# Keys, queries and tokens turned by DMAs instead of TensorE, with the transfers placed around them

## Chip, cores, metric

One core of one Trainium2 chip. The metric is the device time of one execution in microseconds; each figure is a median of several runs, and runs are compared in the fast state only. The "span" of a profile runs from its first instruction to its last and is 1.5 to 2 us shorter than the time. The engines are TensorE (PE; its weight loads PEld), VectorE (DVE), ScalarE (ACT), GpSimd (POOL) and SyncE (SP), which here only issues DMAs.

## The reference, cut

```python
# q, k, v: (4 batches, 8 heads, 768, 64); mem_k, mem_v: (4, 8, 8, 64)
for c in range(24):                              # chunks of 32 queries
    k_ctx = k[:, :, max(0, 32*c - 16) : min(768, 32*c + 40)]   # 16 left, 8 right; v_ctx alike
    scores = q_c @ concat(mem_k, k_ctx).T / 8
    out[c] = softmax(scores) @ concat(mem_v, v_ctx)
x = out as (4, 768, 512)
y = x + relu(((x - mean) / sqrt(var + 1e-6) * g_ln) @ w_ch1) @ w_ch2      # 512 -> 2048 -> 512
```

## The kernel before

The 3072 tokens are worked on as 24 tiles of 128, three tiles to a **unit**; batch b is units 2b and 2b + 1. A unit is 28 steps: 16 up steps (`up`, four matmuls of `w_ch1`, then a ReLU that DVE and ACT take in turn) and 12 down steps (`down`, four matmuls of `w_ch2`). Between them stands the attention of the next unit. A table says behind which step each piece is issued; every engine is given its instructions in this order. An instruction that waits holds up those behind it: in the changed kernel (below) DVE stood 6.6 us before one copy, and the ReLU behind that copy, for which TensorE waited 4.5 us, ran only after it.

The matmuls of this program read three things turned from rows to columns: keys and queries of each batch, and the normalised tokens of each tile. The kernel before does all of it on TensorE, through PSUM, with a copy by DVE or ACT behind each turn:

```python
def turn_kq(pv, src, j, n):              # keys or queries: two heads of a batch
    for r in range(8):
        for par in range(2):
            nc.tensor.matmul(out=pv[64*par : 64*par+64, n*r : n*r+n], lhsT=src[0:n, 2*j+par, r, :],
                             rhs=identity[0:n, 0:n], is_transpose=True, ...)

def turn_x(u, i, t, kind="att"):         # one tile of normalised tokens
    pv = ...                             # PSUM
    for dt in range(4):
        nc.tensor.matmul(out=pv[:, 128*dt : 128*dt+128], lhsT=xn[t % 3][:, 128*dt : 128*dt+128],
                         rhs=identity, is_transpose=True, ...)
    nc.scalar.copy(out=xT[u % 2][:, :, 128*i : 128*i+128], in_=...)
```

Its plan for the units that matter (cut):

```python
elif u in (2, 4):
    attend(((1, 8, 8, 12), (4, 8, 10, 14), (11, 17, 17, 21)))   # scores, values, norm, token turn
    b = u // 2 + 1
    for j, step in ((0, 17), (2, 23)):
        at(step, kq_block, b, j, 0, NG, "mm")                   # keys and queries of batch b
        ...
    for h in range(H):
        at(2 + 2 * h, load_v_head, b, h)                        # values of batch b
    at(21, mem_cols, b); at(21, v_mem, b); at(22, v_around, b)
elif following:
    attend(((12, 17, 17, 21), (14, 17, 17, 22), (18, 23, 23, 26)))
    if u == 3: ...                                              # loads of keys and queries, batch 3
```

`v_around` copies, in SBUF, the rows that neighbouring groups share; it needs all eight value loads.

The softmax here doesn't subtract the row's maximum and nothing guards it: scores larger than these inputs give would overflow.

## Time and profile before

| | before |
|---|---|
| time | 231.92 us (231.57 to 233.25, 3 runs) |
| TensorE busy | 222.8 of 230.2 us |
| units 2 to 6 | 27.1, 24.1, 27.1, 24.1, 24.1 us, TensorE idle 0.0 in each |
| granted clock | 1.0 throughout |

A unit's length is taken from its first up matmul to that of the next. With TensorE idle 0.0 us in units 2 to 6, the account below takes what was removed from it at its length there and each new wait at its own.

### The profile page before, as it was taken

To read this page: it belongs to the slowest core of one execution; us is meant where nothing else is said; L and a number is where in the kernel's file an instruction comes from. 1 tells how busy PE (TensorE), PEld (TensorE's weight loads), DVE (VectorE), ACT (ScalarE), POOL (GpSimd) and SP (SyncE) were. 2 spreads that over 40 slices of the span, in tenths; PEclk is the share of its full clock that TensorE was granted. 3 is DMA by queue.
4 is the path that set the end of the run, shared out by engine and by line. 5 is a ranking of instruction groups with operands and counts; after the bars stand their busy time and mean duration, and the time that the engine had idled before them with its cause. 6 is when DMAs were issued, how large, how long until landed. Compare 5 with 4: busy or idle time off the path is not lost.

```text
span 230.2 us, 5499 instructions
## 1 busy us (share of the span) xinstructions
PE 222.8 (97%) x2289; PEld 138.2 (60%) x2289; DVE 125.4 (54%) x290; ACT 119.0 (52%) x228; POOL 68.6 (30%) x125
## 2 busy tenths in 40 slices
PE   7989999899999999999999999999999999999993
PEld 2455776447765577555765577556765566557553
DVE  5746881475747639575336648674436542663222
ACT  3565648253894576655355367654356335534200
POOL 6973343877360380530001370410001200030000
PEclk9999999999999999999999999999999999999999
DMA  5999999999999999548921199543001200111012
GB/s 80 169 90 203 201 211 150 125 200 226 121 69 126 226 145 36 37 77 119 236 48 48 48 127 23 37 99 106 0 3 46 90 4 0 47 48 46 0 48 93
DMA packets 50307, 21.91 MB, mean 95 GB/s; under 512 B 37817, under 2 KB 46777, under 8 KB 50234
## 3 DMA queue, kind: packets, MB, share of 16 engines
q0 software_dynamic: 45680, 14.23, 90.1%
q1 hardware_dynamic: 4602, 7.33, 10.5%
q8 instruction: 18, 0.29, 0.6%
q14 instruction: 7, 0.06, 0.1%
HBM read 28.48 MB, written 6.29 MB: 151 GB/s over the span
## 4 chain that ended last, share of the span: by engine, by line
PE 77%; DMA 16%; POOL 2%; DVE 2%; issue 1%; POOLq 0%
PE mm L319 32%; PE mm L336 32%; DMA w2c<-in_moe_w_ch_dram 13%; PE att L238 4%; DMA V<-in_v_dram 3%; PE att L258 3%; PE att L176 3%; PE att L296 2%; POOL V L114 2%; PE mm L354 2%; PE mm L176 1%; DVE QZ L374 1%; DVE V L379 0%; DVE V L378 0%; DVE osb L359 0%
## 5 line engine op out<-in xcount | busy, mean ns | idle before, releaser
L319 PE MATMUL mm<-xT,w1c 128*128 128x384 f16 x512 | 88.3, 326 | 0.0
L336 PE MATMUL mm<-w2c,rT 128*128 128x512 f16 x368 | 87.4, 379 | 0.2 <-DMA w2c<-in_moe_w_ch_dram 0.2
L319 PEld LDWEIGHTS <-w1c 128*128 128x128 f16 x512 | 57.0, 114 | 24.2 <-issue 0.3
L327 DVE TENSOR_SCALAR rT<-mm 128x384 f16<-128x384 f32 x64 | 35.5, 556 | 35.3 <-PE mm L319 35.1
L336 PEld LDWEIGHTS <-rT 128*128 128x128 f16 x368 | 33.8, 98 | 34.0 <-issue 0.3
L325 ACT ACTIVATE rT<-mm 128x384 f16<-128x384 f32 x64 | 31.2, 489 | 35.9 <-PE mm L319 33.9
L245 ACT ACTIVATE AT<-att,band 96x512 f16<-96x512 f32 x48 | 30.1, 677 | 17.1 <-PE att L238 16.6
L287 POOL TENSOR_SCALAR veps<-squares 128x1 f32<-128x1 f32 x24 | 4.5, 188 | 109.9 <-ACT junk L284 95.1
L343 DVE SCALAR_TENSOR_TENSOR osb<-mm,rstd,xs 128x512 f32<-128x512 f32 x23 | 17.2, 749 | 30.9 <-PE mm L336 20.4
L114 POOL DMA_DIRECT2D V<-in_v_dram x24 | 21.5, 900 | 15.5 <-DMA V<-in_v_dram 4.5
L301 ACT COPY xT<-att 128x512 f16<-128x512 f16 x21 | 12.2, 581 | 23.8 <-PE att L296 23.8
L191 DVE COPY KT<-att 128x80 f16<-128x80 f16 (+3 forms) x44 | 18.4, 480 | 2.1 <-PE att L176 2.1
L278 DVE SCALAR_TENSOR_TENSOR xn<-xs,nmean,g_row 128x512 f16<-128x512 f32 x24 | 18.0, 752 | 0.9
L201 ACT COPY QZ<-mm 64x768 f16<-64x768 f16 (+1 forms) x18 | 13.6, 757 | 8.0 <-PE mm L176 7.8
L268 DVE RECIPROCAL rec<-att 128x8 f32<-128x8 f32 x24 | 4.9, 203 | 23.3 <-PE att L258 23.3
L284 ACT ACTIVATE junk<-xs,nmean 128x512 f16<-128x512 f32 x24 | 17.4, 724 | 0.1
L269 DVE SCALAR_TENSOR_TENSOR xs<-att,rec 128x512 f32<-128x512 f32 x24 | 16.6, 691 | 0.8
L238 PE MATMUL att<-QZ,KT 128*128 128x128 f16 x192 | 14.8, 219 | 0.9 <-ACT AT L245 0.6
L238 PEld LDWEIGHTS <-KT 128*128 128x128 f16 x192 | 12.6, 98 | 4.6 <-issue 1.4
L201 ACT COPY QZ<-att 64x384 f16<-64x384 f16 (+1 forms) x20 | 12.0, 598 | 5.3 <-PE att L176 5.1
L291 POOL TENSOR_TENSOR rstd<-veps,mhalf 128x1 f32<-128x1 f32 x24 | 13.3, 553 | 2.0
L258 PEld LDWEIGHTS <-AT 96*64 96x64 f16 x384 | 7.9, 111 | 8.7 <-issue 6.0
(63 smaller groups left out, 145.5 us busy)
## 6 DMA issues: line engine op xcount, KB each, us to landing
out_dram<-osb SPq DMA_DIRECT2D x23, 256.0 KB, 5.9
w1c<-in_moe_w_ch_dram POOLq DMA_DIRECT2D x4, 512.0 KB, 12.0
w2c<-in_moe_w_ch_dram POOLq DMA_DIRECT2D x4, 512.0 KB, 15.7
V<-in_v_dram POOLq DMA_DIRECT2D x20, 88.0 KB, 14.1
k<-in_k_dram POOLq DMA_DIRECT2D x2, 768.0 KB, 12.4
q<-in_q_dram POOLq DMA_DIRECT2D x2, 768.0 KB, 16.1
V<-in_v_dram POOLq DMA_DIRECT2D x16, 96.0 KB, 5.9
k<-in_k_dram POOLq DMA_DIRECT2D x3, 256.0 KB, 6.3
```

The lines of the kernel that those rows point to most:

```text
L114: nc.gpsimd.dma_start(out=V[b % 2][r : r + hi - lo, g, :, 0:64], in_=dram(v, b * H * HS + lo * D, [[64, hi - lo], [HS, H], [1, 64]]),)
L191: copy(out=free(KT[b % 2], j * KC + 24 + 32 * ga + 8 * lo, [[KR, gb - ga], [8, m], [1, 8]]), in_=free(pv, lo, [[8, gb - ga], [1, m], [n, 8]]),
L201: copy(out=free(QZ[b % 2][rows, j, g0, par, :], 0, [[128, g1 - g0], [8, 8], [1, 8]]), in_=free(pv[rows, :], 8 * g0, [[8, g1 - g0], [1, 8], ...
L238: nc.tensor.matmul(out=p[:, gg, 128 * j : 128 * j + 128], lhsT=KT[b % 2][:, j, KR * g : KR * g + 128], rhs=QZ[b % 2][:, j, g, :, :], start ...
L245: nc.scalar.activation(out=free(a, 32 * c, [[512, 2], [64, 8], [1, 32]], KR), in_=free(p, 32 * c, [[512, 2], [64, 8], [1, 32]], KR), func= ...
L278: nc.vector.scalar_tensor_tensor(out=xn[i], in0=x, scalar=nmean[i], in1=g_row, op0=ALU.add, op1=ALU.mult,)
L284: nc.scalar.activation(out=junk, in_=xs[xi], func=ACTF.Square, bias=nmean[i], accum_out=squares[i],)
L319: nc.tensor.matmul(out=p, lhsT=free(w, i, [[4, 128]]), rhs=xT[u % 2][:, dt, 0 : 128 * n], start=(dt == 0), stop=(dt == 3),)
L325: nc.scalar.activation(out=o, in_=p, func=ACTF.Relu)
L327: nc.vector.tensor_scalar(out=o, in0=p, scalar1=0.0, scalar2=None, op0=ALU.max)
L336: nc.tensor.matmul(out=p, lhsT=rT[hc][:, 128 * i : 128 * i + 128], rhs=w2c[hc // 4][:, hc % 4, :], start=(hc == 0), stop=(hc == 15),)
L343: nc.vector.scalar_tensor_tensor(out=o, in0=p, scalar=rstd[t % 9], in1=xs[t % 9], op0=ALU.mult, op1=ALU.add,)
```

## The change

Its intent is to take the turns of keys and queries of batches 2 and 3, and of the tokens of units 3 to 7, off TensorE: DMAs on the SP queue (`dma_start_transpose`, DMA_TRANSPOSE in the traces; here called turns on the crossbar) read rows from SBUF and write them turned to SBUF. For that, keys and queries are loaded as tokens (128 rows of 256 B for each of 8 heads), a unit ahead; the crossbar turns stand in the stretches where the plan has no value loads; DVE then spreads the queries, and POOL copies the neighbours' key columns. The core of the diff, with cuts:

```diff
+    def load_tokens(b, which, t):
+        dst, src = ((kraw[0], k), (qraw[0], q))[which]
+        nc.gpsimd.dma_start(out=free(dst, 512 * t, [[64, H], [1, 64]]),
+            in_=dram(src, b * H * HS + 128 * t * D, [[D, 128], [HS, H], [1, 64]]))
+    def cross_k(b, half, t0, t1):
+        nc.sync.dma_start_transpose(out=free(KT[b % 2], ...),
+            in_=kraw[0][64 * half : 64 * half + 64, 512 * t0 : 512 * t1])
     def turn_x(u, i, t, kind="att"):
+        if kind == "dma":
+            nc.sync.dma_start_transpose(
+                out=xT[u % 2][:, :, 128 * i : 128 * i + 128], in_=xn[t % 3])
+            return
 ...
         elif u == 1:
-            for which in range(2):
-                at(1, load_kq, 2, which)
+            for t in range(6):
+                for which in range(2):
+                    at(14, load_tokens, 2, which, t)
 ...
         elif following:
-            attend(((12, 17, 17, 21), (14, 17, 17, 22), (18, 23, 23, 26)))
+            attend(((9, 14, 14, 14), (11, 14, 15, 15), (16, 20, 20, 20)))
+            if u == 2:
+                cross((0, 0, 1, 1), 2, 0, 4, 3)           # first turns of batch 2
+                at(9, mem_cols, 2); at(9, k_around, 2, 0, 4)
+                cross((21, 23, 24, 27), 2, 4, 6, 6)       # second turns
+                spread(12, 2, 0, 3)
+            elif u == 3:
+                for h in range(H): at(0, load_v_head, 2, h)
+                at(6, k_around, 2, 4, 6)
+                spread(7, 2, 3, 6)
+                at(10, v_mem, 2); at(10, v_around, 2)
+                ...                                       # at(20, load_tokens, 3, which, t)
+            elif u == 4:
+                for h in range(H): at(0, load_v_head, 3, h)
+                at(18, v_mem, 3); at(18, v_around, 3)
+                at(19, mem_cols, 3)
+                cross((21, 23, 24, 27), 3, 0, 4, 3)
+            elif u == 5:
+                ...                                       # second turns and spreads of batch 3
```

The tokens of unit 2 stay on TensorE. The rest of the diff lays the key and value tiles out anew, and moves one small matmul of the prologue.

More of the change, by code (lines that the diff above doesn't have):

```diff
@@ L34 @@
     KR = 96
-    KC = NG * KR + 32
     HD = 65
@@ L58 @@
     w2c = [sb.tile([128, 4, 512], FP16, name=f"w2c{i}") for i in range(4)]
-    k16 = [sb.tile([96, H, 8, 64], FP16, name=f"k16_{i}") for i in range(2)]
-    q16 = [sb.tile([96, H, 8, 64], FP16, name=f"q16_{i}") for i in range(2)]
+    kraw = [sb.tile([128, 4096], FP16, name=f"kraw{i}") for i in range(2)]
+    qraw = [sb.tile([128, 4096], FP16, name=f"qraw{i}") for i in range(2)]
+    QT = sb.tile([128, NG * 4 * 64], FP16, name="QT")
+    k16 = [t[0:96, 0:4096].rearrange("p (h r d) -> p h r d", h=H, r=8) for t in kraw]
+    q16 = [t[0:96, 0:4096].rearrange("p (h r d) -> p h r d", h=H, r=8) for t in qraw]
     V = [sb.tile([128, NG, H, HD], FP16, name=f"V{i}") for i in range(2)]
-    KT = [sb.tile([128, 4, KC], FP16, name=f"KT{i}") for i in range(2)]
-    QZ = [sb.tile([128, 4, NG, 2, 64], FP16, name=f"QZ{i}") for i in range(2)]
+    KT = [sb.tile([128, NG * 4 * KR + 32], FP16, name=f"KT{i}") for i in range(2)]
+    QZ = [sb.tile([128, NG, 4, 2, 64], FP16, name=f"QZ{i}") for i in range(2)]
     AT = [sb.tile([128, 2, H, 64], FP16, name=f"AT{i}") for i in range(3)]
@@ L112, in load_v_group @@
         lo, hi = max(64 * g - 16, 0), min(64 * g + 72, S)
-        r = 24 + lo - 64 * g
+        r = 16 + lo - 64 * g
         nc.gpsimd.dma_start(
@@ L120, in load_v_head @@
         nc.gpsimd.dma_start(
-            out=V[b % 2][24:88, :, h, 0:64],
+            out=V[b % 2][16:80, :, h, 0:64],
             in_=dram(v, (b * H + h) * HS, [[64, 64], [64 * 64, NG], [1, 64]]),
@@ L127, in v_around @@
         vt = V[b % 2]
-        nc.sync.dma_start(out=vt[8:24, 1:NG, :, :], in_=vt[72:88, 0 : NG - 1, :, :])
-        nc.sync.dma_start(out=vt[88:96, 0 : NG - 1, :, :], in_=vt[24:32, 1:NG, :, :])
+        nc.sync.dma_start(out=vt[0:16, 1:NG, :, :], in_=vt[64:80, 0 : NG - 1, :, :])
+        nc.sync.dma_start(out=vt[80:88, 0 : NG - 1, :, :], in_=vt[16:24, 1:NG, :, :])
     def v_mem(b):
@@ L133, in v_mem @@
         nc.sync.dma_start(
-            out=V[b % 2][0:8, :, :, :],
+            out=V[b % 2][88:96, :, :, :],
             in_=bass.AP(tensor=src.tensor, offset=src.offset,
@@ L166, in mem_cols @@
         nc.vector.tensor_copy(
-            out=free(KT[b % 2], 0, [[KC, 4], [KR, NG], [1, 8]]),
+            out=free(KT[b % 2], KR - 8, [[KR, 4], [4 * KR, NG], [1, 8]]),
             in_=bass.AP(tensor=src.tensor, offset=src.offset,
@@ L191, in keep_k @@
                 copy(
-                    out=free(KT[b % 2], j * KC + 24 + 32 * ga + 8 * lo,
-                             [[KR, gb - ga], [8, m], [1, 8]]),
+                    out=free(KT[b % 2], (4 * ga + j) * KR + 16 + 8 * (lo - 8 * ga),
+                             [[4 * KR, gb - ga], [8, m], [1, 8]]),
                     in_=free(pv, lo, [[8, gb - ga], [1, m], [n, 8]]),
@@ L201, in keep_q @@
         copy(
-            out=free(QZ[b % 2][rows, j, g0, par, :], 0, [[128, g1 - g0], [8, 8], [1, 8]]),
+            out=free(QZ[b % 2][rows, g0, j, par, :], 0, [[512, g1 - g0], [8, 8], [1, 8]]),
             in_=free(pv[rows, :], 8 * g0, [[8, g1 - g0], [1, 8], [n, 8]]),
@@ L230, in keep_rest, with place, cross_q, k_around @@
         kept_later.pop(0)()
+    def place(b, g):
+        return g if b < 2 else g % 2 * (NG // 2) + g // 2
+    def load_tokens(b, which, t):
+        dst, src = ((kraw[0], k), (qraw[0], q))[which]
+        nc.gpsimd.dma_start(
+            out=free(dst, 512 * t, [[64, H], [1, 64]]),
+            in_=dram(src, b * H * HS + 128 * t * D, [[D, 128], [HS, H], [1, 64]]),
+        )
+    def cross_k(b, half, t0, t1):
+        nc.sync.dma_start_transpose(
+            out=free(KT[b % 2], (24 * half + 4 * t0) * KR + 16, [[KR, 4 * (t1 - t0)], [1, 64]]),
+            in_=kraw[0][64 * half : 64 * half + 64, 512 * t0 : 512 * t1],
+        )
+    def cross_q(half, t0, t1):
+        nc.sync.dma_start_transpose(
+            out=free(QT, (24 * half + 4 * t0) * 64, [[64, 4 * (t1 - t0)], [1, 64]]),
+            in_=qraw[0][64 * half : 64 * half + 64, 512 * t0 : 512 * t1],
+        )
+    def k_around(b, t0, t1):
+        kt, a = KT[b % 2], max(t0, 1)
+        own = lambda half, t: (24 * half + 4 * t) * KR
+        for dst, src, m, w in (
+            (own(1, t0), own(0, t0) + 64, t1 - t0, 16),
+            (own(0, a), own(1, a - 1) + 64, t1 - a, 16),
+            (own(0, t0) + 80, own(1, t0) + 16, t1 - t0, 8),
+            (own(1, a - 1) + 80, own(0, a) + 16, t1 - a, 8),
+        ):
+            nc.gpsimd.tensor_copy(
+                out=free(kt, dst, [[KR, 4 * m], [1, w]]), in_=free(kt, src, [[KR, 4 * m], [1, w]])
+            )
+    def spread_q(b, half, t0, t1):
+        for par in range(2):
+            rows = slice(64 * par, 64 * par + 64)
+            nc.vector.tensor_copy(
+                out=QZ[b % 2][rows, 6 * half + t0 : 6 * half + t1, :, par, :],
+                in_=QT[rows, (24 * half + 4 * t0) * 64 : (24 * half + 4 * t1) * 64].rearrange(
+                    "p (t j x) -> p t j x", j=4, x=64),
+            )
     def scores(b, t):
@@ L235, in scores @@
         for gg in range(2):
-            g = 2 * t + gg
+            g = place(b, 2 * t + gg)
             for j in range(4):
@@ L239, in scores @@
                     out=p[:, gg, 128 * j : 128 * j + 128],
-                    lhsT=KT[b % 2][:, j, KR * g : KR * g + 128],
-                    rhs=QZ[b % 2][:, j, g, :, :],
+                    lhsT=KT[b % 2][:, (4 * g + j) * KR : (4 * g + j) * KR + 128],
+                    rhs=QZ[b % 2][:, g, j, :, :],
                     start=True, stop=True,
@@ L293, in turn_x @@
     def turn_x(u, i, t, kind="att"):
+        if kind == "dma":
+            nc.sync.dma_start_transpose(
+                out=xT[u % 2][:, :, 128 * i : 128 * i + 128], in_=xn[t % 3]
+            )
+            return
         pv = as16(slot("att")[:, 0, :]) if kind == "att" else as16(slot("mm")[:, :])
@@ L368, in clear_k @@
     def clear_k(i):
-        nc.vector.memset(KT[i][:, :, 8:24], 0.0)
-        nc.vector.memset(KT[i][:, :, NG * KR - 8 : KC], 0.0)
+        end = 4 * KR * (NG - 1)
+        nc.vector.memset(free(KT[i], 0, [[KR, 4], [1, 16]]), 0.0)
+        nc.vector.memset(free(KT[i], end + 80, [[KR, 4], [1, 8]]), 0.0)
+        nc.vector.memset(KT[i][:, end + 4 * KR : end + 4 * KR + 32], 0.0)
     def clear_q(i, par):
@@ L406 @@
             load_kq(0, which, 0, CUT, h, h + 4)
-    keep(counts[:, 0:1], counts[:, 0:1], 24, 0.0)
-    keep(counts[:, 1:2], counts[:, 1:2], -88, 0.0)
+    keep(counts[:, 0:1], counts[:, 0:1], 16, 0.0)
+    keep(counts[:, 1:2], counts[:, 1:2], -80, 0.0)
     make_identity(nc, identity)
@@ L417 @@
     mem_cols(0)
-    pg = slot("mm")[:, :]
-    nc.tensor.matmul(out=pg, lhsT=ones32, rhs=g_one, start=True, stop=True)
-    nc.scalar.copy(out=g_row, in_=pg)
+    stay_busy(4)
     v_mem(0)
@@ L427 @@
     nc.gpsimd.memset(zero2[:, 1:2], -NEG)
-    keep(band[:, 0:1], zero2[:, 0:1], -64, NEG)
-    keep(band[:, 1:2], zero2[:, 0:1], 40, NEG)
-    keep(zero2[:, 1:2], zero2[:, 1:2], -8, 0.0)
-    nc.gpsimd.tensor_tensor(out=band[:, 1:2], in0=band[:, 1:2], in1=zero2[:, 1:2], op=ALU.add)
+    keep(band[:, 0:1], zero2[:, 0:1], -56, NEG)
+    keep(band[:, 1:2], zero2[:, 0:1], 32, NEG)
+    keep(zero2[:, 1:2], zero2[:, 1:2], 88, 0.0)
+    nc.gpsimd.tensor_tensor(out=band[:, 0:1], in0=band[:, 0:1], in1=zero2[:, 1:2], op=ALU.add)
     for g in range(4, 6):
@@ L480 @@
     scores(0, 1)
-    stay_busy(5)
+    stay_busy(2)
+    pg = slot("mm")[:, :]
+    nc.tensor.matmul(out=pg, lhsT=ones32, rhs=g_one, start=True, stop=True)
+    nc.vector.tensor_copy(out=g_row, in_=pg)
+    stay_busy(1)
     values(0, 0)
@@ L509, in at, with attend @@
             plan.setdefault(step, []).append((fn, args))
-        def attend(steps):
+        def attend(steps, kind="dma"):
             for i, (s0, s1, s2, s3) in enumerate(steps):
@@ L517, in attend, with cross, spread @@
                 at(s2, norm, t % 6, t % 9)
-                at(s3, turn_x, u + 1, i, t % 6)
-                at(min(s3 + 1, 27), root, t % 6, t % 9)
-        late = ((16, 19, 19, 22), (17, 21, 21, 24), (19, 23, 23, 26))
+                at(s3, turn_x, u + 1, i, t % 6, kind)
+                at(min(s3 + 3, 27), root, t % 6, t % 9)
+        def cross(steps, b, t0, t1, t2):
+            for half in range(2):
+                at(steps[half], cross_k, b, half, t0, t1)
+                at(steps[2 + half], cross_q, half, t2 - 3, t2)
+        def spread(step, b, t0, t1):
+            for half in range(2):
+                at(step + half, spread_q, b, half, t0, t1)
         if u == 0:
@@ L534 @@
                 at(15, load_v_group, 1, g)
-            attend(late)
+            attend(((16, 19, 19, 22), (17, 21, 21, 24), (19, 23, 23, 26)), "att")
             at(26, mem_cols, 1)
@@ L543 @@
                 at(0, load_v_group, 1, g)
-            for which in range(2):
-                at(1, load_kq, 2, which)
-            attend(late)
-        elif u in (2, 4):
-            attend(((1, 8, 8, 12), (4, 8, 10, 14), (11, 17, 17, 21)))
-            b = u // 2 + 1
-            for j, step in ((0, 17), (2, 23)):
-                at(step, kq_block, b, j, 0, NG, "mm")
-                at(step, keep_rest)
-            for h in range(H):
-                at(2 + 2 * h, load_v_head, b, h)
-            at(21, mem_cols, b)
-            at(21, v_mem, b)
-            at(22, v_around, b)
-        elif following:
-            attend(((12, 17, 17, 21), (14, 17, 17, 22), (18, 23, 23, 26)))
-            if u == 3:
-                for which in range(2):
-                    at(2 + which, load_kq, 3, which)
+            for t in range(6):
+                for which in range(2):
+                    at(14, load_tokens, 2, which, t)
+            attend(((16, 19, 19, 22), (17, 19, 20, 23), (21, 23, 23, 26)), "att")
+        elif following:
+            attend(((9, 14, 14, 14), (11, 14, 15, 15), (16, 20, 20, 20)))
+            if u == 2:
+                cross((0, 0, 1, 1), 2, 0, 4, 3)
+                at(9, mem_cols, 2)
+                at(9, k_around, 2, 0, 4)
+                cross((21, 23, 24, 27), 2, 4, 6, 6)
+                spread(12, 2, 0, 3)
+            elif u == 3:
+                for h in range(H):
+                    at(0, load_v_head, 2, h)
+                at(6, k_around, 2, 4, 6)
+                spread(7, 2, 3, 6)
+                at(10, v_mem, 2)
+                at(10, v_around, 2)
+                for t in range(6):
+                    for which in range(2):
+                        at(20, load_tokens, 3, which, t)
+            elif u == 4:
+                for h in range(H):
+                    at(0, load_v_head, 3, h)
+                at(18, v_mem, 3)
+                at(18, v_around, 3)
+                at(19, mem_cols, 3)
+                cross((21, 23, 24, 27), 3, 0, 4, 3)
+            elif u == 5:
+                at(0, k_around, 3, 0, 4)
+                cross((0, 0, 1, 1), 3, 4, 6, 6)
+                spread(6, 3, 0, 3)
+                at(12, k_around, 3, 4, 6)
+                spread(17, 3, 3, 6)
         for step in range(16 + 4 * n):
```

## The prediction

> **What bounds the kernel now.** I read the page of the kernel before from the top: busy time by engine, then the chain that ended last.
>
> ```profile
> PE 222.8 (97%) x2289; PEld 138.2 (60%) x2289; DVE 125.4 (54%) x290; ACT 119.0 (52%) x228; POOL 68.6 (30%) x125
> ...
> PE 77%; DMA 16%; POOL 2%; DVE 2%; issue 1%; POOLq 0%
> PE mm L319 32%; PE mm L336 32%; DMA w2c<-in_moe_w_ch_dram 13%; PE att L238 4%; DMA V<-in_v_dram 3%; PE att L258 3%; PE att L176 3%; PE att L296 2%; POOL V L114 2%; PE mm L354 2%; PE mm L176 1%; DVE QZ L374 1%; DVE V L379 0%; DVE V L378 0%; DVE osb L359 0%
> ```
>
> TensorE is busy 97% and makes 77% of the chain; the DMA share is the first weights, up to 48.9 us. So a TensorE instruction removed after 48.9 us is worth its own length, if no wait takes its place. To see where that holds I cut the span at the starts of the units (three tiles of 128 tokens each), with the boundaries taken from the chain in order of time.
>
> ```profile
> 48.90:79.40 30.50, 30.48 (x341) 19.00 (x341) 19.41 (x42) 19.57 (x36) 14.12 (x22) 1.00 1.94 157
> 79.40:106.50 27.10, 27.10 (x326) 17.36 (x324) 16.84 (x39) 17.81 (x33) 10.53 (x18) 1.00 1.30 82
> 106.50:130.60 24.10, 24.10 (x199) 14.76 (x197) 11.79 (x26) 10.79 (x22) 1.48 (x4) 1.00 0.53 106
> 130.60:157.70 27.10, 27.10 (x325) 17.36 (x324) 16.84 (x39) 17.77 (x33) 8.91 (x16) 1.00 1.13 74
> 157.70:181.80 24.10, 24.10 (x199) 14.81 (x197) 11.79 (x26) 10.82 (x22) 1.48 (x4) 1.00 0.09 34
> ```
>
> These are start:end, length, then busy us and count of PE, PEld, DVE, ACT and POOL, granted clock, DMA share, GB/s. TensorE is full to the hundredth in each. Units 2 and 4 are 3.0 us longer than 3 and 5: they turn the keys and queries of batches 2 and 3. The chain around the first of these:
>
> ```profile
> 94.63 0.68 PE att L176 x32
> 95.32 0.68 PE mm L176 x32
> 96.00 3.56 PE mm L336 x16
> 99.56 0.22 PE att L296 x4
> 99.78 1.73 PE mm L336 x8
> 101.50 0.80 PE att L176 x32
> 102.31 0.68 PE mm L176 x32
> ```
>
> Start, length, what. L176 turns keys and queries, L296 turns the normalised tokens.
>
> [...] The trace has 219 ns for the TensorE turn[...]; no crossbar turn is in it. [...] one output store, landing time last, at the end of the kernel with nothing beside it and at 107.5 us beside key and query loads:
>
> ```profile
> out_dram<-osb SPq DMA_DIRECT2D x1, 256.0 KB, 2.0
> ...
> out_dram<-osb SPq DMA_DIRECT2D x1, 256.0 KB, 7.6
> ```
>
> **The change part by part.** *Removed from TensorE:* the four L176 runs of a batch, 0.68 + 0.68 + 0.80 + 0.68 = 2.84 us, twice: 5.7 us. The token turns of units 3 to 7, 15 groups of four at 0.22 us (one 0.35): 3.4 us. Sum **9.1 us**, all on the path. With no new wait: 231.9 - 9.1 = 222.8.
>
> *Removed beside the path:* the copies out of PSUM, 5.2 us of DVE and 6.4 us of ACT per batch, and 15 copies of 0.58 us on ACT. Neither engine limits, so nothing.
>
> *Added:* 16 small DVE copies that spread the queries, 16 POOL copies for the neighbour keys, 8 crossbar turns of keys and 8 of queries (0.13 to 0.26 MB each), 15 of tokens (0.13 MB). All crossbar turns stand in the SP queue, in order, with output stores and the copies around the values. *Moved:* the 24 loads of keys and queries now fetch rows of 256 B (1024 a load) where they fetched 2 KB; the eight value loads of a batch start a unit later. *Prologue:* two filler matmuls more, one copy from ACT to DVE; the stretch before 48.9 us also waits for weights, so about nothing.
>
> **The rival: new waits.** What such rows cost, from the value loads of the kernel before (group of issues with median landing; then the POOL timeline):
>
> ```profile
> V<-in_v_dram POOLq DMA_DIRECT2D x6, 96.0 KB, 6.9
> ...
> 80.77 4.48 POOL L120 DMA_DIRECT2D V<-in_v_dram  x6
> ```
>
> Six loads of 768 rows, issued in 4.5 us, the last landing 7.1 us after its issue at 84.5: about 91.6, or 10.9 us in all. [...] A token load is then 1.3 to 1.9 us, twelve of them 15 to 22 us. I walked the built program's order, with 0.65 us per up step (four L319), 0.86 per down step (four L336), 0.45 per scores, 0.33 to 0.4 per values.
>
> (a) *Unit 2.* Values of batch 1 land until 75.8 us as now; the seventh token load, the last that the first key turn needs, at about 85 to 88. Two key turns and two query turns follow[...]. DVE meets the spread at step 12, 88.7 us, and is stuck there; the scores at step 16 (92.7 us) need an accumulator that DVE frees only after spread and norm, 2 us later. TensorE then waits 1 to 7 us; I take 2.5.
>
> (b) *Unit 3.* POOL reaches the value loads of batch 2 once the third tile's root is done, about 3 us before unit 3 starts. Eight loads need about 11 to 14 us, the copies around them, which wait for all eight, about 3 more: ready 11 to 14 us into the unit. The first values stand at step 14, 10.7 us in. Wait 0 to 4, more if the crossbar turns run beside them; I take 3.
>
> (c) *Token turns.* The third tile's normalised rows are ready about 3.7 us before its unit starts. [...] Unit 4's runs beside the token loads of batch 3; the store above lost 5 us in such company. I take 1.5 over all units.
>
> (d) *Unit 5.* Twelve token loads then eight value loads of batch 3 start 6.6 us before unit 4 and need 25 to 36 us. The copies around the values wait for them in the SP queue at step 18 of unit 4, ahead of the third token turn for unit 5, needed 23 us into unit 4. With fast loads nothing is lost, with slow ones 5 or more; I take 2.
>
> Sum 9: 222.8 + 9 = **231.8 us**.
>
> *Second rival: all transfers stay hidden.* For it: the page's DMA row is 0 to 4 tenths in most slices after 140 us, and the steps of spread and norm look placed from traces. Then 223 to 226. *Third rival: DVE, ACT or POOL becomes the bound.* Against it: units 3 and 5 keep TensorE full with DVE at 11.8 of 24.1 us, ACT at 10.8, POOL at 1.5; the POOL copies add some us but have units of room. Worth nothing in time.
>
> **Range and chances.** All hidden gives about 223.5; all four waits at their upper ends, 7 + 5 + 4 + 5 = 21, gives about 243. Faster by over 2% means under 227.3, so at most 4.5 us of waits: 0.30. Within 2% allows 4.5 to 13.8 us of waits, where my sum lies: 0.38. Slower, the rest: 0.32, because several of these waits share one cause, the load rate, and would come together.
>
> **What would show it.** TensorE busy should fall by about 9 us to some 214 in any case; ACT falls by about 21, DVE by 10 less the spread. Idle TensorE before L288 (scores) in unit 2, after a DVE copy that waited for a query turn, would confirm (a); before L308 (values) in unit 3, released by the copy of values to values, (b); before L374 at a unit's first step, released by a token turn, (c) and (d). Token loads landing 1.3 to 1.9 us apart would confirm the rate. The prediction is wrong on the fast side if the seventh token load lands before 83 us[...]; on the slow side if a crossbar turn next to loads takes several times its time alone, since every turn, store and copy behind it in the SP queue is then late.

## The result

The changed kernel took **242.06 us** (median of 4 runs, one of them slow), the kernel before 231.75. Ratios are the mean time of one kernel's fast runs over that of the other's of the same rounds, so not quite the ratio of these medians: 1.0423, with a 95% interval of 1.0348 to 1.0499. It is slower.

The page of the changed kernel, with the lines that answer to those of before: busy time, TensorE and its granted clock over 40 slices of the span, and the chain.

```profile
PE 219.4 (92%) x1975; PEld 130.7 (54%) x1975; DVE 122.2 (51%) x285; ACT 99.9 (42%) x196; POOL 90.8 (38%) x161
...
PE   7888999899999998997469989993999999999994
...
PEclk9999999999999999999779999997699999999999
...
PE 63%; DMA 28%; DVE 3%; issue 2%; POOL 1%; SPq 1%; ACT 0%; ACTq 0%
PE mm L391 29%; PE mm L374 26%; DMA V<-in_v_dram 15%; DMA qraw<-in_q_dram 5%; DMA xT<-xn 4%; PE att L288 3%; PE att L308 3%; DMA QT<-qraw 2%; DMA V<-V 2%; PE mm L409 1%; PE att L178 1%; SPq L253 1%; POOL V L116 1%; POOL V L122 1%; DVE xs L319 1%
```

314 matmuls are gone, yet TensorE's busy time fell by 3.4 us only, and the chain now passes through value loads, token turns and value copies. The second and third row say why busy time misleads: where TensorE had gaps (4 and 6, 3 tenths), its clock fell to about 0.7 of full speed (digits 7 and 6) in the slices at the gaps or behind them. The table by stage, units 2 to 6, in the columns explained in the prediction:

```profile
79.15:103.61 24.46, 23.51 (x185) 14.01 (x184) 13.50 (x31) 10.58 (x22) 7.77 (x18) 1.00 0.73 102
103.61:138.61 35.00, 26.98 (x186) 14.81 (x185) 14.03 (x31) 9.94 (x20) 12.79 (x22) 0.90 1.28 103
138.61:166.15 27.54, 23.52 (x184) 14.04 (x185) 12.13 (x27) 9.94 (x20) 12.19 (x20) 0.97 2.65 123
166.15:192.28 26.13, 26.11 (x184) 14.63 (x184) 13.86 (x33) 9.98 (x20) 4.45 (x14) 0.90 0.57 110
192.28:215.64 23.36, 23.36 (x186) 14.04 (x184) 11.87 (x26) 9.94 (x20) 2.21 (x6) 1.00 0.17 52
```

Unit 6 shows what the change is worth undisturbed: 23.36 us. In the other units, length less PE busy is idle time: 1.0, 8.0, 4.0 and 0.0 us. Units 3 and 5 also have 3.6 and 2.8 us more *busy* time than the same instructions take in unit 6, at a clock of 0.90. The account of units 2 to 6, cut at the same places in both traces, closes:

| | us |
|---|---|
| before, units 2 to 6 | 126.4 |
| turns taken off TensorE (126.4 less 5 x 23.36 us undisturbed) | -9.6 |
| new idle time, units 2 to 5 (1.0 + 8.0 + 4.0 + 0.0) | +13.0 |
| slower matmuls in units 3 and 5 (3.6 + 2.8) | +6.4 |
| busy time over 23.36 us in units 2 and 4 | +0.3 |
| after | 136.5 |

What TensorE waited for in unit 3, from the list of waits (total, times, longest):

```profile
PE mm L374 <- DVE rT L382: 4.6, 2, 4.5
PE att L308 <- DMA V<-V: 2.3, 1, 2.3
PE mm L374 <- DMA xT<-xn: 1.1, 1, 1.1
```

The first wait is for a ReLU that DVE did late. DVE's instructions in order of time (start, length, what, idle time before and what ended it) show why:

```profile
108.36 0.56 DVE L382 TENSOR_SCALAR rT<-mm 128x384 f16<-128x384 f32 x1 [0.74 <-PE mm L374]
115.56 0.72 DVE L276 COPY QZ<-QT 64x768 f16<-64x768 f16 x2 [6.64 <-DMA QT<-qraw]
116.31 0.56 DVE L382 TENSOR_SCALAR rT<-mm 128x384 f16<-128x384 f32 x1
118.45 0.72 DVE L276 COPY QZ<-QT 64x768 f16<-64x768 f16 x2 [1.58 <-DMA QT<-qraw]
```

DVE stood 6.6 us before the second spread of batch 2, which waited for a query turn, and the ReLU stood behind it. Other transfers were on their way at this time:

```profile
V<-in_v_dram POOLq DMA_DIRECT2D x8, 96.0 KB, 8.7
out_dram<-osb SPq DMA_DIRECT2D x2, 256.0 KB, 11.2
KT<-kraw SPq DMA_TRANSPOSE x2, 7.4
QT<-qraw SPq DMA_TRANSPOSE x2, 11.1
```

(Last column: us from issue to landing, of the issues from 100 to 108 us whose landing is known.) POOL had issued the eight value loads at 100.7 us, before unit 3 began, since nothing in its order held it back; they met the second turns of batch 2, issued on SP from 101.0 us. So the plan's "between" did not come about. The last value load landed at 117.7, the copies around the values at 123.0; the first values matmul came at 123.1 us.

In unit 4 the remaining 4.0 us are a wait for the third token turn of unit 5: issued at 161.7, landed at 166.1. It stood in the SP queue behind copies (159.1 us) that had waited for the value loads of batch 3.

### The profile page after: what moved, and what is told of

The parts are those of the page before. It is cut to its first block, busy times and chain, and to the rows that moved or that the text cites. A ratio compares the mean times of both kernels' runs of the same rounds, so it can differ in the third digit from the quotient of the medians.

```text
span 239.8 us, 4938 instructions
## 1 busy us (share of the span) xinstructions
PE 219.4 (92%) x1975; PEld 130.7 (54%) x1975; DVE 122.2 (51%) x285; ACT 99.9 (42%) x196; POOL 90.8 (38%) x161
## 4 chain that ended last, share of the span: by engine, by line
PE 63%; DMA 28%; DVE 3%; issue 2%; POOL 1%; SPq 1%; ACT 0%; ACTq 0%
PE mm L391 29%; PE mm L374 26%; DMA V<-in_v_dram 15%; DMA qraw<-in_q_dram 5%; DMA xT<-xn 4%; PE att L288 3%; PE att L308 3%; DMA QT<-qraw 2%; DMA V<-V 2%; PE mm L409 1%; PE att L178 1%; SPq L253 1%; POOL V L116 1%; POOL V L122 1%; DVE xs L319 1%
## 5 line engine op out<-in xcount | busy, mean ns | idle before, releaser
L374 PE MATMUL mm<-xT,w1c 128*128 128x384 f16 x512 | 92.7, 338 | 9.8 <-DMA xT<-xn 5.1
L391 PE MATMUL mm<-w2c,rT 128*128 128x512 f16 x368 | 85.8, 382 | 0.0
L374 PEld LDWEIGHTS <-w1c 128*128 128x128 f16 x512 | 57.6, 115 | 38.9 <-issue 15.7
L391 PEld LDWEIGHTS <-rT 128*128 128x128 f16 x368 | 34.8, 98 | 37.5 <-issue 0.9
L116 POOL DMA_DIRECT2D V<-in_v_dram x24 | 21.5, 897 | 14.1 <-DMA w1c<-in_moe_w_ch_dram 3.9
L308 PE MATMUL att<-V,AT 96*64 96x65 f16 x384 | 10.3, 197 | 4.1 <-DMA V<-V 2.3
L268 POOL COPY KT<-KT 128x128 f16<-128x128 f16 (+4 forms) x16 | 4.4, 306 | 25.2 <-DMA KT<-kraw 25.2
L122 POOL DMA_DIRECT2D V<-in_v_dram x16 | 12.0, 772 | 0.0
L365 PE MATMUL mm<-busy 128*128 128x512 f16 x34 | 10.5, 431 | 1.2 <-DVE counts L455 1.2
```

The costliest lines, as they stand in the source:

```text
L116: nc.gpsimd.dma_start(out=V[b % 2][r : r + hi - lo, g, :, 0:64], in_=dram(v, b * H * HS + lo * D, [[64, hi - lo], [HS, H], [1, 64]]),)
L308: nc.tensor.matmul(out=p[64 * gg : 64 * gg + 64, h // 4, c0 : c0 + HD], lhsT=AT[t % 3][0:KR, gg, h, :], rhs=V[b % 2][0:KR, 2 * t + gg, h, ...
L374: nc.tensor.matmul(out=p, lhsT=free(w, i, [[4, 128]]), rhs=xT[u % 2][:, dt, 0 : 128 * n], start=(dt == 0), stop=(dt == 3),)
L391: nc.tensor.matmul(out=p, lhsT=rT[hc][:, 128 * i : 128 * i + 128], rhs=w2c[hc // 4][:, hc % 4, :], start=(hc == 0), stop=(hc == 15),)
```

## The experiments

All are edits of the changed kernel unless stated otherwise; all gave right results. The first four shared a chip and its runs of the kernel before (median 232.0 us).

**Values early.** Moves the value loads of batch 2 from unit 3 to unit 2, ahead of the second turns.

```diff
-                for h in range(H):          # u == 3
-                    at(0, load_v_head, 2, h)
+                for h in range(H):          # u == 2, behind k_around at 9
+                    at(10, load_v_head, 2, h)
```

> The changed kernel with one part undone: the eight value loads of batch 2 are issued in unit 2 (step 10, behind the first neighbour copies on POOL) instead of at the start of unit 3, so that the second set of crossbar turns has no loads beside it. Theory (the value loads of batch 2 run beside the second crossbar turns, each makes the other late, and TensorE waits first for the spread queries and then for the values): both waits of unit 3 (4.6 and 2.3 us) go, and so does the half clock behind them, 3.5 us; unit 3 falls from 34.8 to about 24 us, the kernel from 242 to about 231. The eight loads land in 13 us or less. Rival (the crossbar turns are slow by themselves and the spread stands too early): the wait for the queries stays at 3 us or more, the kernel gains under 4 us.

Measured: 234.17 us, ratio 1.0105 (1.006 to 1.0151), 3 us above the 231 expected. Unit 3 fell from 35.0 to 26.0 us at full clock:

```profile
105.40:131.40 26.00, 23.61 (x185) 14.00 (x186) 13.50 (x31) 9.95 (x20) 9.95 (x17) 1.00 0.82 107
```

So the meeting of these loads with the second turns costs about 8 of the 10 us. It did not reach 231, because the loads now met something else, the first two token turns. First line: the two turns issued in unit 2 of this run, beside value loads; second: the same two of the changed kernel, beside nothing (last column: us to landing):

```profile
xT<-xn SPq DMA_TRANSPOSE x2, 8.1
...
xT<-xn SPq DMA_TRANSPOSE x2, 2.4
```

Both turns beside the loads landed 0.3 and 0.8 us behind the last value load (103.8 and 104.3 against 103.5), and the trace has no packet of the hardware queue from 92 to 100 us although both had been issued by 97. Here the turns were not slowed in proportion; they were held until the loads were nearly through. It is not a rule: in the changed kernel, from 110 to 112 us, 378 packets of the hardware queue moved beside 512 of the value loads' queue. The eight loads took 15.4 us, not the 13 or less expected.

**Spread late.** Moves only what blocked DVE.

```diff
-                spread(7, 2, 3, 6)
+                spread(22, 2, 3, 6)
```

> The changed kernel with the second spread of batch 2 moved from step 7 to step 22 of unit 3, so DVE is not blocked by late query turns. Theory (two waits in a row, and the later one, for the values, sets the end): the 4.6 us wait before the up matmuls goes, the wait for the values grows from 2.3 to about 8 us, the kernel stays within 2 us of 242. Rival (the DVE stuck behind the spread is the cause of unit 3's loss): the kernel gains 6 us or more and the wait for the values stays near 2 us.

Measured: 242.72 us, ratio 1.0467 (1.039 to 1.0544), as the theory had it. The wait for the ReLU is gone and that for the values took its place:

```profile
PE att L308 <- DMA V<-V: 8.7, 1, 8.7
PE mm L374 <- DMA xT<-xn: 5.0, 2, 4.2
```

The largest wait in the list of the changed kernel, 4.5 us for DVE, was thus worth nothing: behind it stood a later one.

**Around late.** Puts the copies around the values of batch 3 behind the third token turn.

```diff
-                at(18, v_mem, 3)
-                at(18, v_around, 3)
+                at(20, v_mem, 3)
+                at(20, v_around, 3)
```

> The changed kernel with the copies around the values of batch 3 put behind the third token turn of unit 4 on the SP queue (step 20 instead of 18), nothing else. Theory (the turn is late only because it stands behind copies that wait for the value loads): the 4.0 us wait at the start of unit 5 goes and with it the half clock of 2.9 us; the kernel is about 7 us faster, 235. Rival (the turn is slow because of the value loads that run beside it): it still lands 4 us or more after its issue and 2 us or more of the wait stay; gain under 4 us.

Measured: 247.08 us, ratio 1.0613 (1.0529 to 1.0697): slower, against both expectations. Its profiled run fell in the slow state, and unit 3, which the edit doesn't touch, had 39.8 us there; so only units 4 and 5 are read, and only for their waits:

```profile
144.70:168.07 23.37, 23.37 (x185) 14.04 (x185) 11.38 (x26) 9.95 (x20) 11.60 (x20) 1.00 2.93 120
168.07:199.42 31.35, 25.65 (x185) 15.04 (x184) 14.62 (x34) 10.04 (x20) 4.38 (x14) 0.89 0.61 108
```

The wait before unit 5 is gone whole, so the turn had been late by its place behind the copies: in the changed kernel its rows were ready at 157.9 us and it was issued at 161.7, here it was issued as soon as its rows were ready. But unit 5 now has 5.7 us of idle time, all before scores that wait for spread queries: the first turns of batch 3 stand behind the same copies now, and their spread stands at step 6. The two units together are 1.0 us longer than in the changed kernel (54.7 against 53.7). The wait was moved, not removed. That 1.0 us is less than the 4.3 us by which the fast runs are longer on average (246.1 against 241.8); where the rest lies is not shown, since the one profile is of a slow run.

**Filler.** Puts 16 matmuls on zeros into the wait at the end of unit 4.

```diff
+                at(27, fill, 16)     # u == 4; fill: stay_busy(16) on an idle PSUM tile
```

> The changed kernel with 16 matmuls on zeros, about 3.5 us of TensorE work that no result needs, put into the wait at the end of unit 4. Theory (the idle time itself takes half of the clock away for the next microseconds): the granted clock stays 1.0 through unit 5, whose length falls from 26.3 to about 23.4 us; the kernel is about 2.5 to 3 us faster although it does more work. Rival (the clock falls for another reason, such as the transfers or the load of the chip): unit 5 stays at 26.3 us, the kernel is the same or slower.

The clock first. In the changed kernel, the stretches of one microsecond around that wait (start:end, length, TensorE busy, granted clock, DMA share, GB/s):

```profile
162.00:163.00 1.00, 0.13 (x1) 1.00 0.87 233
163.00:164.00 1.00, 0.00 (x0) 1.00 0.47 109
164.00:165.00 1.00, 0.00 (x0) 0.81 1.34 146
165.00:166.00 1.00, 0.00 (x0) 0.50 0.92 158
...
170.00:171.00 1.00, 1.00 (x5) 0.50 0.89 184
171.00:172.00 1.00, 1.00 (x7) 0.78 0.98 282
172.00:173.00 1.00, 1.00 (x8) 1.00 0.90 149
```

TensorE went idle at 162.1; the clock halved at about 164.6, and was whole again only at about 171.4, 5.3 us after work resumed. In units 2 to 6 of the profiled runs the stretches at half clock lasted 3.4 us (twice in unit 3 of the changed kernel, once in values early), 6.8 (here) and 10.2 (in spread late). The length of the wait did not set the price: waits of 4.2 us at this same place left 2.9 us of work at half clock in values early and 2.6 in spread late, against 5.3 behind 4.0 us here. In values early work resumed at 159.1:

```profile
158.00:159.00 1.00, 0.00 (x0) 0.81 0.98 170
159.00:160.00 1.00, 0.89 (x3) 0.50 0.91 209
160.00:161.00 1.00, 1.00 (x5) 0.50 0.97 244
161.00:162.00 1.00, 1.00 (x5) 0.50 0.88 148
162.00:163.00 1.00, 1.00 (x8) 0.98 0.65 119
```

With the filler, unit 5 stayed at 1.00:

```profile
168.06:193.03 24.97, 23.68 (x185) 14.08 (x185) 14.02 (x33) 9.99 (x20) 4.38 (x14) 1.00 0.63 115
```

Its busy time fell from 26.11 to 23.68 us, 2.4 us less for the same instructions: here the idle time itself took the clock away. The kernel as a whole was not faster (243.08 us; ratio 1.0495, 1.0425 to 1.0565): 1.3 us came back as a wait for spread queries in unit 5, and unit 3, not touched, was 1.2 us longer in this run (36.2 us; 35.0 in the changed kernel and 39.8 in around late, with the same code up to there). The expected gain in time was a miss, the cause was a hit.

The next two ran on the same chip (before 231.99 us).

**Windows.** Lays all transfers anew: a second raw buffer for batch 3; value loads of batch 2 in unit 1; value loads of batch 3 behind the key copies in unit 4; turns of keys and queries behind the third token turn.

```diff
+            # u == 1: value loads of batch 2 at 1;  u == 2: token loads of batch 2 at 0, v_around at 5
+                cross((21, 21, 22, 22), 2, 0, 4, 3)                    # u == 2
+            # u == 3: k_around at 3, token loads of batch 3 at 4, spread at 7
+                cross((21, 21, 22, 22), 2, 4, 6, 6)                    # u == 3
+            # u == 4: k_around at 0, value loads of batch 3 at 1, spread at 6, v_around at 13
+                cross((21, 21, 22, 22), 3, 0, 4, 3)                    # u == 4
+            # u == 5: k_around at 3, spread at 7, last turns at 9 and 10, k_around at 12, spread at 17
```

> All the parts of the changed kernel, with the transfers laid anew: value loads of batch 2 in unit 1 ahead of the token loads, token loads of batch 3 into the second raw buffer in unit 3, its value loads at the start of unit 4, the crossbar turns of keys and queries behind the third token turn of a unit, and every spread at least 8 steps behind its turns. Theory (the change loses only by transfers that meet, and by the half clock behind the waits): idle TensorE in units 2 to 5, 13 us in the changed kernel, falls under 3 us, no unit's clock falls under 0.98, time 222 to 226 us, 2 to 4% under the kernel before. Rival (there isn't enough room for the transfers in any order): two or more units keep waits over 1.5 us, and the time is 229 us or more.

Measured: 228.07 us, ratio 0.9844 (0.9799 to 0.9888), clock 1.00 in all units. It is faster clear of noise, but by 1.6% where 2 to 4% were expected, and the time lies between the ranges of both expectations. The clock came as the theory had it; idle time is 1.1, 0.8, 1.4 and 1.8 us in units 2 to 5, 5.1 us together where under 3 was expected: 2.8 us for spread queries, 2.3 us for token turns. There is room, but no slack.

**Tokens only.** The kernel *before*, with only the token turns of units 3 to 7 moved.

```diff
 # before:
+        if kind == "dma": nc.sync.dma_start_transpose(out=xT[...], in_=xn[t % 3]); return
-            attend(((1, 8, 8, 12), (4, 8, 10, 14), (11, 17, 17, 21)))          # u in (2, 4)
+            attend(((1, 8, 8, 8), (4, 8, 10, 10), (11, 17, 17, 17)))
-            attend(((12, 17, 17, 21), (14, 17, 17, 22), (18, 23, 23, 26)))
+            attend(((9, 14, 14, 14), (11, 14, 15, 15), (16, 20, 20, 20)))
```

> One part alone: the kernel before, with keys and queries still turned on TensorE, loads as before, and only the tokens of units 3 to 7 turned on the crossbar. Theory (a token turn costs TensorE nothing where no value loads run beside it in its last 4 us): the 3.4 us of TensorE time come out nearly whole, 228 to 229 us, ratio 0.985 to 0.99; turns that are issued beside value loads land 5 us or more later, the others in 2 to 3 us. Rival (the third turn of a unit is late by itself): each of units 3 to 7 starts with a wait of 0.5 us or more and the time stays at 231 to 233 us.

Measured: 227.20 us, ratio 0.9819 (0.9767 to 0.987), just under the 228 to 229 expected; faster clear of noise, though whether by 2% is open. Units 2 to 5 have 26.3, 23.4, 26.3 and 23.4 us and no idle time at all: the turned tokens give their whole 0.7 to 0.8 us a unit. About 1.4 us more of the gain lie in unit 0, where the profiled run waited 1.0 us less. The edit only delays the variances there, and unit 0 took 27.8 to 29.6 us in the profiles of the changed kernel and the first four experiments, where its code is the same: so this part may be chance. The expectation that turns beside value loads land after 5 us or more was not met: the longest landing known in this run is 4.1 us.

**Batch 3 only.** On another chip, with 5 rounds (before 231.54 us): tokens, and the keys and queries of batch 3, on the crossbar; batch 2 on TensorE with its loads of before.

```diff
+            # u == 2 as in the kernel before, token turns at 8, 10 and 17
+            # u == 3: token loads of batch 3 at 2, into the second raw buffer
+                cross((21, 21, 22, 22), 3, 0, 4, 3)                    # u == 3
+            # u == 4: value loads at 0, k_around at 9, v_around at 13 (ahead of the first token turn)
+                cross((21, 21, 22, 22), 3, 4, 6, 6); spread(24, 3, 0, 3)      # u == 4
+            # u == 5: k_around at 3, spread at 17
```

> A version meant to beat both kernels: tokens of units 3 to 7 and the keys and queries of batch 3 alone turned on the crossbar; batch 2 turned on TensorE with the 2 KB loads of the kernel before. The batch-3 token loads go into the second raw buffer in unit 3, its value loads at the start of unit 4, its turns behind the third token turn of units 3 and 4, its spreads 8 steps or more behind. Theory (each turned part is worth its TensorE time where its transfers find room): the 227.2 us of the tokens alone less the 2.8 us that batch 3 costs on TensorE, 224 to 225 us, ratio about 0.97, idle TensorE under 1 us from unit 2 on, clock 1.0. Rival (the room is used up by the tokens' turns): idle TensorE of 2 us or more in units 4 and 5 and a time of 227 us or more.

Measured: **225.04 us**, ratio 0.9711 (0.966 to 0.9762), faster than both kernels. Units 2 to 4:

```profile
78.59:104.89 26.30, 26.30 (x313) 16.69 (x312) 16.82 (x39) 16.41 (x30) 15.01 (x23) 1.00 1.37 95
104.89:128.26 23.37, 23.37 (x186) 14.02 (x184) 11.87 (x26) 9.95 (x20) 10.35 (x16) 1.00 1.39 124
128.26:151.62 23.36, 23.36 (x186) 14.03 (x185) 13.37 (x31) 9.95 (x20) 6.37 (x15) 1.00 1.80 137
```

TensorE is full in each, as in the kernel before, with fewer instructions.

## Why the prediction was right or wrong, point by point

- **The time** lies in the range, 242.1 in 223.5 to 243, but 10.3 us above the 231.8 that the sum gave, and the likeliest class did not come (slower had 0.32, the same 0.38). That the range held is partly luck: its upper end stood for 21 us of waits (222.8 + 21 is 243.8), and what came was 13.0 us of waits and 6.4 us of half clock, for which it had no term. The mechanism, four new waits against a fixed gain, was right; two of the waits, (b) and (d), were taken too small, (a) and (c) too large, and one cause was missing.
- **The gain of 9.1 us** was nearly right: units 2 to 6 less five undisturbed units is 9.6. Keys and queries took 3.06 us a batch (27.11 less 24.05), not the 2.84 of the sum. The two other kernels that reached 0.0 idle confirm it part by part. (The 219 ns in the prediction are the length of one turn; turns overlap, and four together took 0.22 us.)
- **(a), unit 2, taken as 2.5: measured 1.0.** The 1 to 7 us from which the 2.5 were taken rest on the author's estimate of a turn on the crossbar; no trace before the change has such a turn. The seventh token load landed at 78.9, not at 85 to 88 us. The 1.0 us stands where the prediction put it: before scores, behind a spread that waited 1.1 us for a query turn. Token loads landed 0.9 us apart on average (73.4 for the first, 83.6 for the twelfth, 11 gaps), no slower than POOL issued them (1.05 us apart), not 1.3 to 1.9; in windows those of batch 2 landed 1.4 apart. The rate was the author's estimate, taken from value loads (the 10.9 us measured for 4608 rows are 2.4 us for 1024). Value loads were slower row for row: 768 rows in 1.5 us on average in values early, and in 1.8 beside turns in the changed kernel, against 1024 rows in 0.9 to 1.4. The cause was not shown; no run varied the layout that the loads write.
- **(b), unit 3, taken as 3: measured 6.9 of idle time ahead of the values, and 3.6 through the clock.** The place and the cause were right. The step "eight loads need about 11 to 14 us, the copies about 3 more" failed: from the first issue at 100.7 the loads took 17.0 us and the copies, issued at 117.9, 5.0 (the 3 us were the author's estimate; no landing of such copies is known in the trace of the kernel before). Values early has 15.4 us for the eight loads without the second turns beside them, so the turns account for 1.6 us of it, and the estimate was low without any company. The spread at step 7 of unit 3 was not looked at; it took up most of the wait but, as spread late shows, did not set it.
- **(c), token turns, taken as 1.5: measured 1.1,** at the start of unit 4, beside token loads: 5.1 us to landing instead of 2.4. Right here; in windows two token turns beside token loads took 6.8 and 8.1 us. What sets the time beside other loads was not shown.
- **(d), unit 5, taken as 2: measured 4.0 and 2.8 through the clock.** The cause, a turn behind copies in the SP queue, was right, and around late shows it; that those copies would be missed elsewhere if moved was not foreseen.
- **The half clock** is the missing term, 6.4 us of the 10.3 that the point estimate was short; it is also why TensorE's busy time did not fall to "some 214 in any case" but only to 219.4. In the changed kernel the stretches at half clock (0.50) lasted 3.4, 3.4 and 6.8 us. They began 4.4, 2.8 and 2.5 us after TensorE went idle, and in filler one began after 2.1. Waits of 2.3 us (changed kernel, unit 3) and 2.2 us (filler, unit 3) were enough, both begun about 0.6 us after the clock had come back from an earlier drop. The profile of the kernel before, with its clock of 1.0 throughout, has no such stretch to read it from. A prediction that sums waits of this length on TensorE has to add it, and mine did not.
- **The rivals.** "All transfers stay hidden" is refuted for this order of transfers, and shown for another (batch 3 only). "DVE, ACT or POOL becomes the bound" is refuted as put: none is over 14.1 us in a unit of the changed kernel from unit 2 on. DVE mattered not by its load but by standing in front of a late transfer.

## What to carry to other kernels

A plan by steps fixes only the order within an engine: here the loads of an engine with nothing before them were issued 2.9 us before their unit began, and met what they were meant to follow. Take work off the bounding engine piece by piece, and give each transfer a place where nothing that the bound waits for stands behind it, in its queue or on an engine that blocks in order; here half of the change gave 2.9%, and the whole cost 4.2%. When waits on TensorE are in the sum, look at what the clock adds behind them: in units 2 to 6 of these runs, waits of up to 1.4 us left the clock whole, and all of 2.2 us and more did not; in the changed kernel it added 3.6 us in unit 3 and 2.8 us in unit 5.
